# Joining Q and the selection in one DMA transpose, pairing the score rows of batch 0, and reordering the loads of a chunk-selecting attention kernel

## The chip, the cores and the metric

The kernel runs on one core of a Trainium2 chip. The metric is device time in microseconds (us) of one execution; each figure below is the median of several executions, with the range where it matters. Every execution has a state; nearly all of those here are fast, the few slow ones are left out of the ratios, and only fast runs are compared. Engine names: PE is TensorE's matmuls and PEld its weight loads, DVE is VectorE, ACT is ScalarE, POOL is GpSimd, SP is SyncE, which issues most of the transfers. The profile itself is one execution, so its span differs by a microsecond or two from the median.

## The reference

Four batches, eight heads, 768 positions, head size 64. K is cut into 24 chunks of 32 positions. For each query an upper bound of its score with each chunk is formed from the chunk's minimum and maximum, and only the best six chunks are attended to. The result goes through a gated feed-forward layer.

```python
k_min, k_max = k_chunks.min(axis=3), k_chunks.max(axis=3)
ub = sum(maximum(q * k_min, q * k_max), axis=-1)          # 24 bounds for each query
ub = where(causal, ub, -1e9)
top_chunks = argsort(ub)[..., -6:]
scores = where(chunk_of_key in top_chunks and key <= query, q @ k.T / 8, -1e9)
x = softmax(scores) @ v                                   # 3072 tokens x 512
out = (relu(x @ w_gate) * (x @ w_val)) @ w_out            # 512 -> 1536 -> 512
```

## The kernel before

The work is split into 16 attention jobs, one for each batch and pair of heads, and six feed-forward units of 512 tokens. The two are interleaved, so that TensorE does feed-forward matmuls while the other engines prepare the next job. The first 128 positions of each batch need no selection and form a "first block" of their own.

A planner written in Python orders every operation before the program is built. It simulates the engines with estimated costs and takes, whenever an engine comes free, the ready operation of best priority. The order that results is fixed: each engine then works through its queue in order. An operation that waits holds up everything behind it in that queue, so a wrong estimate in the planner becomes a real wait on the chip.

```python
op("SP", 1.25, prio, f, after=after, makes=makes, take=take, hold=hold, lag=2.6)  # a DMA transpose
...
if ok and (best is None or (ops[i][2], i) < (ops[best][2], best)):                # the choice: by priority
    best = i
```

In this form a DMA transpose is, for the planner, 1.25 us of SyncE and a result 2.6 us later; it does not take time on the DMA queue, although loads do (an operation on "DMA").

The mask of the selection is added by TensorE itself. A score matmul contracts 128 rows: 64 rows of K against Q, and in the other 64 rows a one-hot table of chunks, `ind`, with a large negative value, against the transposed "not selected" flags. Both operands of it, `kx[h]` and `qx[h]`, are therefore put together from halves:

```python
for h in range(2):                                  # K: two half copies for a job
    copy_half(eng[h], n, ..., kx[h][64*h:64*h+64], kT, h, ...)
for h in range(2):                                  # Q: two half copies
    copy_half(eng[h], n, ..., qx[h][64*h:64*h+64], qT, h, ...)
sT = turned(sn, ..., lambda: sel, nr, on_pe, ...)   # the selection, transposed
for h in range(2):                                  # and copied to the other halves
    copy_half(eng[h], nr*128, ..., qx[1-h][64*h:64*h+64], sT, h, ...)
...
nc.tensor.matmul(t[:, h, o:o+m*128], kx[h][:, c*128:(c+1)*128],
                 qx[h][:, (qb-1)*128:(qb-1+m)*128], ...)
```

K, Q and the attention output x are transposed on TensorE in batches 0 and 1 and by DMA in batches 2 and 3; the selection too. K and Q of batches 0 and 1 are loaded in long runs (eight positions of a head in one piece), those of batches 2 and 3 in short ones (one position). The feed-forward weights come in four equal groups, issued by GpSimd:

```python
WIDE = lambda b: b < 2            # long runs
PE_KQ = PE_SEL = PE_X = lambda b: b < 2
for i in range(4):
    weights(("w", i), [gate part i, value part i], (-28.0, -7.9, -7.8, -7.7)[i],
            after=[(("ld","v",-1),("ld","q",0),("ld","q",1),("ld","q",2))[i]])   # a landing
for i in range(4):
    weights(("wo", i), [output part i], (4.0, 5.0, 6.0, 7.0)[i], after=[("ld","v",3)])
```

The softmax here doesn't subtract the row's maximum and nothing guards it: scores larger than these inputs give would overflow.

## Time and profile before

| | before |
|---|---|
| median of 4 runs | 309.53 us (308.92 to 310.26) |
| profiled execution, span | 308.1 us |
| TensorE busy | 274.3 us |
| VectorE, ScalarE, GpSimd busy | 184.3, 178.1, 91.9 us |

The profile of before, first part: busy time of each engine, with its share of the span and its instructions.

```profile
PE 274.3 (89%) x2230; PEld 148.5 (48%) x2268; DVE 184.3 (60%) x524; ACT 178.1 (58%) x242; POOL 91.9 (30%) x164
```

Second part of the same page: the span in 40 slices of 7.7 us. The digits are tenths: busy share of TensorE, its granted clock, busy share of the DMA engines.

```profile
PE   2841998967998998999999899999999999999994
...
PEclk9995899995999999999999999999999999999999
DMA  9999999999899779986662264231100110020002
```

TensorE is full from the eleventh slice on. Ahead of that it has holes, the DMA engines are full, and the granted clock falls to half twice: 22.6 to 32.8 us and 70.4 to 77.2 us in the trace's clock records. The Trainium skill, "TensorE: Matmul & The Clock Gate", Part 1, says that the clock is halved after an idle window of about 3.4 us; here the clock did fall (0.50 granted), but without a single hole that long ahead of it. The stretches are 10.24 and 6.83 us long, multiples of 3.41 us. In the 3.41 us before the first, TensorE was busy 1.17 us, and its longest hole was 1.5 us; in the 3.41 us before the second it was busy 0.82 us, and the holes there are 2.6 and 2.2 us long. The 6.0 us wait shown below falls inside the first stretch. So shorter holes close together were enough. What they cost is their idle time and the work at half clock after them.

Stretches of before. Columns: the stretch and its length; busy time and instructions of PE, PEld, DVE, ACT, POOL; mean granted clock; DMA share (the time that packets took, over the time of 16 engines; packets overlap, so it can pass 1); GB/s.

```profile
0.00:80.00 80.00, 56.09 (x521) 32.29 (x530) 50.85 (x150) 39.69 (x53) 40.54 (x68) 0.89 1.20 210
80.00:120.00 40.00, 37.02 (x366) 21.45 (x371) 36.74 (x96) 33.56 (x47) 19.34 (x33) 1.00 0.92 180
120.00:180.00 60.00, 57.69 (x576) 33.89 (x585) 52.16 (x178) 47.97 (x61) 22.42 (x43) 1.00 0.69 129
180.00:220.00 40.00, 39.68 (x391) 23.02 (x396) 23.01 (x74) 31.18 (x40) 9.54 (x23) 1.00 0.33 70
220.00:320.00 100.00, 83.80 (x382) 37.83 (x387) 21.51 (x32) 25.67 (x43) 0.00 (x0) 1.00 0.09 34
```

TensorE idles 23.9 us of the first 80, 3.0 of the next 40 and 2.3 of the 60 after that. The last row runs past the end of the span (308.1), so its idle time is 88.1 - 83.8 = 4.3 us.

What TensorE waited for in before: total us, times, longest.

```profile
PE g L793 <- DMA wg_61<-in_moe_w_gate_dram: 6.0, 1, 6.0
...
PE yp L828 <- DMA wo_69<-in_moe_w_out_dram: 2.6, 1, 2.6
PE yp L828 <- DMA wo_70<-in_moe_w_out_dram: 2.2, 1, 2.2
```

The timeline of before, TensorE and then GpSimd: start, length, engine and line, instruction, and in brackets the wait ahead of it.

```profile
30.17 1.48 PE L793 MATMUL g<-xT,wg_61 128*128 128x512 bf16 x3 [5.96 <-DMA wg_61<-in_moe_w_gate_dram]
...
68.38 0.82 PE L828 MATMUL yp<-wo_69,hT 128*128 128x512 bf16 x3 [2.59 <-DMA wo_69<-in_moe_w_out_dram]
...
16.84 0.91 POOL L850 DMA_DIRECT2D wg_61<-in_moe_w_gate_dram  x1
...
57.58 0.76 POOL L850 DMA_DIRECT2D wo_69<-in_moe_w_out_dram  x1
```

The first gate weights are issued at 16.84 us and are awaited until 30.17; the first output weights are issued at 57.58 and awaited until 68.38. The Trainium skill, "DMA: Bandwidth & Descriptors", section "Issuing engines are not separate DMA queues", says that transfers run on the same 16 engines and interleave whichever engine issued them. That fits the trace: the weights, issued by GpSimd, took 12.9 us to land beside SyncE's loads, while the DMA share stood at 1.2.

### The profile page before, as it was taken

What the parts mean: (1) busy time and instruction counts of PE and PEld (TensorE: products, weight loads), DVE (VectorE), ACT (ScalarE), POOL (GpSimd) and SP (SyncE); (2) the same over time, 40 slices, a digit from 0 to 9 for tenths busy, and PEclk for the clock granted to TensorE, in tenths of its full rate; (3) what the DMA queues carried; (4) which work ended last, traced back from release to release, by engine and by line L of the source; (5) the groups of instructions that cost most, each with busy time, mean ns of one, the idle gap of its engine ahead of it and who ended that gap; (6) DMA issues with size and microseconds to landing.
All of it is one profiled execution on the core that took longest, in us unless ns stands there. A gap on an engine that the chain in (4) does not pass through costs nothing.

```text
span 308.1 us, 5930 instructions
## 1 busy us (share of the span) xinstructions
PE 274.3 (89%) x2230; PEld 148.5 (48%) x2268; DVE 184.3 (60%) x524; ACT 178.1 (58%) x242; POOL 91.9 (30%) x164
## 2 busy tenths in 40 slices
PE   2841998967998998999999899999999999999994
PEld 1431455643565554555655455555544444444441
DVE  7454789952879999978998798523434023204310
ACT  3421378860979794877898788988233223233321
POOL 5594146670555263243533332223000000000000
PEclk9995899995999999999999999999999999999999
DMA  9999999999899779986662264231100110020002
GB/s 168 218 229 222 212 214 227 209 187 231 158 235 242 90 172 186 187 145 137 168 139 49 56 89 80 92 80 54 24 0 0 69 70 0 34 104 1 0 34 102
DMA packets 95389, 37.88 MB, mean 123 GB/s; under 512 B 83840, under 2 KB 89472, under 8 KB 95360
## 3 DMA queue, kind: packets, MB, share of 16 engines
q1 hardware_dynamic: 89536, 32.78, 53.5%
q0 software_dynamic: 5824, 4.72, 9.6%
q8 instruction: 17, 0.28, 0.4%
q14 instruction: 12, 0.10, 0.1%
HBM read 30.41 MB, written 6.29 MB: 119 GB/s over the span
## 4 chain that ended last, share of the span: by engine, by line
PE 58%; DMA 19%; POOL 6%; DVE 5%; issue 5%; ACT 3%; SPq 2%; POOLq 0%; ACTq 0%; DVEq 0%
PE g L793 20%; PE yp L828 19%; DMA vraw<-in_v_dram 7%; PE sT L675 7%; PE vl L793 6%; PE o L726 5%; DMA kraw<-in_k_dram 5%; DMA wo_70<-in_moe_w_out_dram 3%; DMA qT<-qbf 2%; DMA kT<-kbf 2%; POOL aT L698 2%; DVE kmm L552 1%; SPq L380 1%; ACT aT L686 1%; POOL kbf L521 1%
## 5 line engine op out<-in xcount | busy, mean ns | idle before, releaser
L686 ACT ACTIVATE aT<-sT 128x1024 bf16<-128x1024 f32 x80 | 78.7, 1022 | 20.7 <-PE sT L675 16.7
L804 ACT ACTIVATE grl<-g 128x512 bf16<-128x512 f32 x72 | 42.9, 596 | 58.5 <-PE g L793 50.3
L698 POOL TENSOR_SCALAR_AFFINE_SELECT aT<-aT 128x256 bf16<-128x256 bf16 x80 | 32.2, 417 | 63.5 <-ACT aT L686 63.1
L812 DVE TENSOR_TENSOR hT<-vl,grl 128x512 bf16<-128x512 f32 x48 | 33.1, 689 | 21.3 <-PE vl L793 20.2
L828 PEld LDWEIGHTS <-hT 128*128 128x128 bf16 x288 | 27.7, 99 | 37.2 <-issue 3.8
L812 DVE TENSOR_TENSOR hT<-g,grl 128x512 bf16<-128x512 f32 x24 | 16.6, 692 | 45.3 <-ACT grl L804 31.6
L552 DVE TENSOR_REDUCE kmm<-kT 128x24 bf16<-128x768 bf16 x32 | 29.8, 948 | 7.4 <-PE kT L343 7.2
L838 ACT ACTIVATE y<-yp 128x512 f32<-128x512 f32 x24 | 14.4, 598 | 27.3 <-PE yp L828 23.3
L675 PEld LDWEIGHTS <-kx_all 128*128 128x128 bf16 x256 | 21.5, 98 | 14.3 <-issue 1.3
L726 PEld LDWEIGHTS <-aT 128*128 128x128 bf16 x640 | 23.2, 98 | 9.3 <-POOL aT L698 2.7
L793 PE MATMUL g<-xT,wg_61 128*128 128x512 bf16 x69 | 18.5, 390 | 6.1 <-DMA wg_61<-in_moe_w_gate_dram 6.0
L828 PE MATMUL yp<-wo_69,hT 128*128 128x512 bf16 x71 | 19.9, 386 | 3.0 <-DMA wo_69<-in_moe_w_out_dram 2.6
L828 PE MATMUL yp<-wo_70,hT 128*128 128x512 bf16 x70 | 20.3, 400 | 2.2 <-DMA wo_70<-in_moe_w_out_dram 2.2
L828 PE MATMUL yp<-wo_71,hT 128*128 128x512 bf16 x70 | 19.2, 379 | 0.2
L828 PE MATMUL yp<-wo_72,hT 128*128 128x512 bf16 x70 | 19.0, 379 | 0.1
L793 PE MATMUL g<-xT,wg_63 128*128 128x512 bf16 x70 | 18.2, 379 | 0.9 <-ACT grl L804 0.8
L521 POOL CAST kbf<-kraw 96x1024 bf16<-96x1024 f32 (+1 forms) x16 | 15.2, 952 | 11.6 <-DMA kT<-kbf 5.1
L363 DVE COPY kx_all<-kT 64x768 bf16<-64x768 bf16 x24 | 18.2, 759 | 0.4
L793 PE MATMUL g<-xT,wg_62 128*128 128x512 bf16 x70 | 18.2, 379 | 0.2
L793 PE MATMUL g<-xT,wg_64 128*128 128x512 bf16 x69 | 18.2, 379 | 0.1
L521 POOL CAST qbf<-qraw 80x1024 bf16<-80x1024 f32 (+1 forms) x16 | 14.1, 882 | 13.4 <-DMA qT<-qbf 11.5
L741 DVE TENSOR_TENSOR x<-o,zr 128x320 bf16<-128x320 f32 x32 | 15.7, 491 | 1.1
(187 smaller groups left out, 449.7 us busy)
## 6 DMA issues: line engine op xcount, KB each, us to landing
kraw<-in_k_dram SPq DMA_DIRECT2D x16, 384.0 KB, 7.6
vraw<-in_v_dram SPq DMA_DIRECT2D x16, 384.0 KB, 6.4
out_dram<-y SPq DMA_DIRECT2D x24, 256.0 KB, 2.0
qraw<-in_q_dram SPq DMA_DIRECT2D x8, 320.0 KB, 12.2
qraw<-in_q_dram SPq DMA_DIRECT2D x16, 160.0 KB, 3.7
kraw<-in_k_dram SPq DMA_DIRECT2D x4, 256.0 KB, 5.0
qraw<-in_q_dram SPq DMA_DIRECT2D x4, 256.0 KB, 5.0
vraw<-in_v_dram SPq DMA_DIRECT2D x4, 256.0 KB, 5.1
```

Of the source, the lines that this page charges most:

```text
L363: nc.vector.tensor_copy(out=out, in_=i)
L521: nc.gpsimd.tensor_copy(out=new(nm + "bf", bn)[0:np_, 0:ns * 2 * D].rearrange("p (r h d) -> p r h d", h=2, d=D), in_=TL[rn][0:np_, 0:ns * ...
L552: nc.vector.tensor_reduce(out=TL[mm][:, m], in_=i, axis=AX.XY if wide else AX.X, op=o)
L675: nc.tensor.matmul(t[:, h, o:o + m * 128], kx[h][:, c * 128:(c + 1) * 128], qx[h][:, (qb - 1) * 128:(qb - 1 + m) * 128], start=(si == 0), ...
L686: nc.scalar.activation(out=TL[an][:, :, a0:a0 + w], in_=TL[sn][:, :, 0:w], func=ACT.Exp, scale=scale)
L698: nc.gpsimd.affine_select(out=d, in_=d, compare_op=ALU.is_ge, fill=0.0, base=0, channel_multiplier=-1, pattern=[[0, 2], [1, 128]])
L726: nc.tensor.matmul(TL[on][:, r - 1, h - h0, :], TL[an][:, h, o:o + 128], vb[:, h, c, :], start=(i == 0), stop=(i == NP - 1))
L741: nc.vector.tensor_tensor(out=TL[xn][:, :, h0 * D:(h0 + hs) * D].rearrange("p r (h d) -> p r h d", d=D), in0=TL[on][:, :, :, 0:D], in1=TL[ ...
L793: nc.tensor.matmul(ps, w[:, kt, cs], TL[xn][:, kt, :], start=(kt == 0), stop=(kt == KT_ - 1))
L804: nc.scalar.activation(out=new("grl", rn), in_=g, func=ACT.Relu)
L812: nc.vector.tensor_tensor(out=TL[hn][:, nt, :], in0=vv, in1=TL[rn], op=ALU.mult)
L828: nc.tensor.matmul(TL[pn], TL[hn][:, nt, tl * 128:(tl + 1) * 128], wo_sb[nt // NPG][:, nt % NPG, :], start=(nt == 0), stop=(nt == NTI - 1))
```

## The change

The intent is to take copies from VectorE and ScalarE, to fill TensorE's holes at the start, and to make the planner's idea of the DMA queue true. The parts:

1. *Start.* Weight groups of 2, 3, 3 and 4 tiles instead of four of 3; each is released by the issue of a load plus a delay instead of a landing; V of the first blocks comes later; the output weights come in two transfers instead of four.
2. *Pair* (batch 0). K, Q and the selection are copied whole. The scores become two passes of matmuls on half the array's height: K against Q, then `ind` against the selection, one head on each half of the rows.
3. *Join* (batches 1 to 3). GpSimd casts Q into a tile `cb` beside the selection, and one DMA transpose of ten 128x128 blocks writes `qx` directly. No copy of Q or of the selection is left there. K, Q (for the clamps of the bound) and x of batch 1 are still transposed on TensorE.
4. *Loads.* K and Q of batch 1 in short runs like those of batches 2 and 3; Q loads all six blocks in one transfer. x goes into one circular tile.
5. *Planner.* A transpose now takes 0.144 us for each block on the planner's DMA queue; SyncE's operations cost 0.12 us more; transfers are taken in the order in which they become available. It also counts the loads in flight in finer units (six, of which a short-run load takes three; before three, of which it took two).

The core of the diff, with cuts:

```diff
+        if eng == "SP":
+            cost += 0.12
 ...
+                    rank = (at[i] if eng in flow else ops[i][2], i)
 ...
-    WIDE = lambda b: b < 2
+    WIDE = lambda b: b < 1
+    PAIR = lambda b: b < 1
-    PE_SEL = lambda b: b < 2
+    PE_SEL = lambda b: b < 1
 ...
+    WGS = [2, 3, 3, 4]
+    xT = const.tile([128, KT_, XC * 128], BF16)
+    cb_l = [const.tile([128, NQ, 2, 128], BF16, name=f"cb{i}") for i in range(NCB)]
 ...
-            op("SP", 1.25, prio, f, after=after, makes=makes, take=[(tag, name)], hold=hold,
-               lag=2.6)
+            dma_t(nr, prio, f, after, makes, take=[(tag, name)], hold=hold)
+    def dma_t(nr, prio, f, after, makes, take=(), hold=()):
+        made = makes[0]
+        op("SP", 1.25, prio, f, after=after, makes=[("ti", made)], take=take, hold=hold, lag=0.0)
+        op("DMA", 0.144 * nr, prio, None, after=[("ti", made)], makes=makes, ...)
 ...
+            if nm == "q" and not PAIR(b):
+                def f_cb(cb=cb, rn=rn):
+                    for h in range(2):
+                        nc.gpsimd.tensor_copy(out=cb[:, :, h, h * D:h * D + D], in_=src[:, h, 1:])
 ...
+        else:
+            dma_t(2 * NQ, p, lambda: nc.sync.dma_start_transpose(
+                out=qx.rearrange("f r h p -> f (r h) p"), in_=cb...), ...)
 ...
+                if PAIR(b):
+                    for k_, q_, first in ((kx[0], x[:, 0:SQ], True), (ind, x[:, SQ:], False)):
+                        for si, (c, qb, m) in enumerate(bank):
+                            for h in range(2):
+                                hs = slice(64 * h, 64 * h + 64)
+                                nc.tensor.matmul(t[:, h, o:o + m * 128],
+                                                 k_[hs, c * 128:(c + 1) * 128],
+                                                 q_[hs, (qb - 1) * 128:(qb - 1 + m) * 128], ...)
 ...
-                (-28.0, -7.9, -7.8, -7.7)[i], [(("ld","v",-1),("ld","q",0),("ld","q",1),("ld","q",2))[i]])
+                ..., [(("iss","v",-1),("iss","k",0),("iss","v",0),("iss","v",1))[i]], 1.5 if i == 0 else 3.5)
```

## The prediction

> **What bounds the kernel now.** The table of stretches shows two regimes. From 80 us on TensorE is busy 218.2 of 228 us: it is the bound. Before 80 us it is busy only 56.1 us, with a granted clock of 0.50 around 24-32 and 72-76 us, while the DMA share stays at its ceiling (1.18-1.22, about 210 GB/s). So about 24 us, and half-clock time, are lost to loads. The timeline and the waits name the holes: the first gate weights are issued at 16.8 us and land 12.9 us later, so TensorE waits 6.0 us until 30.2 and job 0's selection, behind it in order, runs only at 35.3; the first output weights are issued at 57.6 us, behind a V cast that waits 5.0 us for its load; TensorE idles around 65.7-71.4, then runs at half clock till about 78. From 80 to 120 us VectorE is busy 36.7 and ScalarE 33.6 of 40 us, and 3 us of TensorE idle come from their chain.
>
> **What changes.**
> - Load order and weights: a first weight group of 2 tiles (2/3 of the bytes), gated by the issue of loads instead of a landing; K and Q before V; output weights in two transfers, issued earlier. At the rate of before (about 1.5 MB in 19 us) the first group lands near 23 us instead of 30-32. I estimate 7 us earlier, and most of the 65.7-71.4 hole with its half-clock tail (4-8 us) gone. Against it, batch 1's K and Q are now loaded in short runs, and twelve Q loads bring 384 KB instead of 320.
> - VectorE: batch 0's half copies become whole copies (4 x 0.76 saved), selection copies fall from 10.6 to about 2 us, Q copies (3.2) and half the clamps (2.6) leave; memsets add 2. Net -16 us. ScalarE: Q and selection copies leave (about -20), clamps come (+5.6): about -14. GpSimd: 24 casts into the joined tile, about 0.4 each from the 0.72 us of a 128x640 cast: about +10 on 92.
> - TensorE: 20 selection transposes leave (55 ns apart, -1.1 us). Batch 0's scores become two passes of half-height matmuls. The trace has such pairs: at full clock eight started 30 ns apart, so two run together. But entering costs: the first half-height matmul started 0.45 us after the previous 512-column one, where 0.216 is usual. The Trainium skill, "TensorEngine Tiling (Array Packing)", Key Properties, says a change of tiling mode drains the array; the trace agrees. About 16 entries at 0.2-0.3: +3 to 5 us (estimate).
> - DMA: joined transposes move 10 blocks instead of 5; a 5-block one took 2.7 us to land. I expect 4-6 us, mostly planned for.
>
> **On the critical path.** Start: -8 to -13 us. Middle, through VectorE and ScalarE: -2 to -3. TensorE's own work: +2 to +4. Sum about -9.5.
>
> **Prediction:** 300.5 us, 80% range 293 to 307. Faster by over 2%: 0.70; within 2%: 0.26; slower: 0.04.
>
> **What would show it.** Right: the first gate matmul starts near 23-25 us; the first output matmul waits for weights under 1 us; TensorE's busy time before 80 us rises from 56 to about 66; VectorE total near 168, ScalarE near 164, GpSimd near 102; TensorE's busy time about 275-279; idle after 120 us no larger. Wrong: batch 0's scores taking over 5 us more; TensorE waiting on the joined transpose between 70 and 120 us; GpSimd casts on the chain.
>
> **What would make it wrong.** If the load ceiling only moves the hole later (short-run K and Q crowding out weights), the start gains 3-4 us and the result is about 306. If drains cost little and the start fills fully, 293.

## The result, and the profile after

| | before | after |
|---|---|---|
| median of 4 runs each | 309.53 us | 301.85 us (301.73 to 302.26) |
| ratio, with 95% interval | | 0.9753 (0.9727 to 0.9779) |
| profiled execution, span | 308.1 us | 300.6 us |
| TensorE busy | 274.3 us | 273.4 us |
| VectorE, ScalarE, GpSimd busy | 184.3, 178.1, 91.9 us | 168.3, 162.5, 98.0 us |

A ratio here and below is the mean time of one kernel's fast runs over the mean of the other's fast runs of the same rounds on the same chip, so it is not quite the ratio of the medians. The change makes the kernel 2.5% faster, 1.35 us above the predicted median.

The profile after, first part, and the slices (now 7.5 us each):

```profile
PE 273.4 (91%) x2258; PEld 145.6 (48%) x2292; DVE 168.3 (56%) x482; ACT 162.5 (54%) x222; POOL 98.0 (33%) x186
...
PE   2975796998999999989979899999999999999995
...
PEclk9999998999999999999999999999999999999999
DMA  9999999999799999999999622322000020020002
```

While TensorE works, the half clock is down to one stretch, 50.5 to 53.9 us. The DMA engines, however, now stay full until slice 22 (165 us), where before they had eased from slice 19 on (139 us).

Stretches of after, same columns:

```profile
0.00:80.00 80.00, 62.74 (x663) 34.77 (x671) 55.53 (x165) 44.62 (x59) 44.88 (x81) 0.98 1.15 207
80.00:120.00 40.00, 39.39 (x395) 23.28 (x400) 34.48 (x104) 28.39 (x40) 20.43 (x39) 1.00 1.26 217
120.00:180.00 60.00, 55.11 (x589) 32.78 (x596) 47.40 (x165) 47.39 (x60) 28.68 (x58) 1.00 1.09 180
180.00:220.00 40.00, 39.74 (x269) 20.19 (x273) 12.25 (x23) 18.82 (x26) 3.97 (x10) 1.00 0.20 52
220.00:320.00 100.00, 76.44 (x349) 34.61 (x354) 18.68 (x27) 23.28 (x39) 0.00 (x0) 0.99 0.08 32
```

Read the two tables row by row. TensorE's idle time in the first 80 us falls by 6.65 us. From 80 to 120 us it falls from 3.0 to 0.6; of the waits named there in before, 1.7 us were for copies by VectorE and ScalarE into `kx` and `qx`, and they are gone. From 120 to 180 us it rises from 2.3 to 4.9, and the DMA share rises in the same row from 0.69 to 1.09.

What TensorE waited for in after:

```profile
PE sT L741 <- DMA qx_93<-cb_97: 1.8, 1, 1.8
...
PE sT L741 <- DMA qx_91<-cb_95: 1.5, 2, 1.4
...
PE sT L741 <- DMA qx_92<-cb_96: 1.3, 2, 1.1
```

`sT` are the scores and `qx<-cb` are the joined transposes. Asked of 120 to 180 us alone, the same view lists nothing else: 1.8, 1.5 and 1.1 us, together 4.4 of the 4.9 us that TensorE idles there. These waits did not exist before.

The timeline after, TensorE and GpSimd:

```profile
21.54 1.02 PE L866 MATMUL g<-xT,wg_61 128*128 128x512 bf16 x3
...
36.15 0.39 PE L731 MATMUL sT<-qx_91,kx_all 64*128 64x512 bf16 x2
36.38 0.38 PE L731 MATMUL sT<-qx_91,ind 64*128 64x512 bf16 x2
...
76.48 1.46 PE L901 MATMUL yp<-wo_69,hT 128*128 128x512 bf16 x5
...
13.03 0.89 POOL L923 DMA_DIRECT2D wg_61<-in_moe_w_gate_dram  x1
...
50.94 0.84 POOL L923 DMA_DIRECT2D wo_69<-in_moe_w_out_dram  x1
```

The first gate matmul starts 8.6 us earlier; its weights, a smaller group, land 5.2 us after their issue instead of 12.9. The first output matmul does not wait for weights any more. The half-height matmuls come in pairs: two of 512 columns, one for each head, every 0.22 us.

The transfers without a size in the page's list of issues are the transposes; the last number is the median time from issue to landing. In before:

```profile
kT<-kbf SPq DMA_TRANSPOSE x8, 3.4
qT<-qbf SPq DMA_TRANSPOSE x8, 2.6
...
selT<-sel_78 SPq DMA_TRANSPOSE x3, 2.7
```

In after:

```profile
kT<-kbf SPq DMA_TRANSPOSE x8, 4.3
qT<-qbf SPq DMA_TRANSPOSE x8, 4.2
...
qx_93<-cb_97 SPq DMA_TRANSPOSE x4, 4.2
qx_91<-cb_95 SPq DMA_TRANSPOSE x4, 4.1
```

The joined ones land in 4.1 to 4.2 us (a third group of four, left out here, also in 4.2), and the transposes of K and Q, whose size is the same in the two kernels, have also become slower.

The chain that ended last, from 110 to 172 us of after: start, length, what. Only its transfers are copied.

```profile
110.56 6.06 DMA qx_92<-cb_96
...
129.17 5.63 DMA qx_91<-cb_95
...
146.57 5.40 DMA qx_93<-cb_97
...
156.72 3.62 DMA qx_91<-cb_95
...
166.13 3.48 DMA qx_92<-cb_96
```

These five pieces are 24.2 us of the chain. That is not idle time of TensorE, which does feed-forward work meanwhile; it shows through what the next job's scores come: VectorE's comparison, the joined transpose, the scores, and no copy in between.

Where the 7.5 us between the two profiled spans came from:

| term | measured | how |
|---|---|---|
| idle time before 80 us | -6.65 us | first rows |
| work done at half clock | -2.7 us | busy time at clock 0.50 was 8.9 us, is 3.4; half of the difference (estimate) |
| TensorE's own work, at full clock | +1.9 us | busy time less half of what ran at half clock: 269.8, then 271.7 |
| idle time, 80 to 220 us | +0.15 us | three rows: -2.4, +2.6, -0.1 |
| after 220 us, idle | -0.15 us | last rows, less what lies past the span |

The split is coarse. The ends of matmuls are modelled in the trace, and some records are missing: before's trace has 2230 matmuls, e1's 2268, for the same TensorE work. By the working of the third row, e1 (below) comes to 273.1 us, 3.2 us more than before without any new work on TensorE. A difference of 2 us in that row is therefore no evidence of a cause, and the idle rows share the doubt.

### The profile page after: what moved, and what is told of

Read it like the earlier page. It is cut to its first block, busy times and chain, and to the rows that moved or that the text cites. A ratio compares the mean times of both kernels' runs of the same rounds, so it can differ in the third digit from the quotient of the medians.

```text
span 300.6 us, 5925 instructions
## 1 busy us (share of the span) xinstructions
PE 273.4 (91%) x2258; PEld 145.6 (48%) x2292; DVE 168.3 (56%) x482; ACT 162.5 (54%) x222; POOL 98.0 (33%) x186
## 4 chain that ended last, share of the span: by engine, by line
PE 70%; DMA 18%; DVE 5%; issue 2%; POOL 2%; ACT 1%; SPq 0%; POOLq 0%; ACTq 0%; DVEq 0%
PE g L866 23%; PE yp L901 19%; PE vl L866 9%; PE sT L741 7%; PE o L793 6%; DMA qraw<-in_q_dram 5%; DMA kraw<-in_k_dram 5%; DMA qx_92<-cb_96 3%; DMA qx_91<-cb_95 3%; DMA qx_93<-cb_97 2%; PE sT L731 2%; DVE hT L885 1%; PE kT L367 1%; PE xt L367 1%; PE ub L651 1%
## 5 line engine op out<-in xcount | busy, mean ns | idle before, releaser
L753 ACT ACTIVATE aT<-sT 128x1024 bf16<-128x1024 f32 x80 | 79.6, 1026 | 23.4 <-PE sT L741 15.7
L901 PE MATMUL yp<-wo_70,hT 128*128 128x512 bf16 x141 | 34.8, 379 | 0.2
L901 PE MATMUL yp<-wo_69,hT 128*128 128x512 bf16 x137 | 34.3, 379 | 0.4
L741 PEld LDWEIGHTS <-kx_all 128*128 128x128 bf16 x192 | 16.0, 98 | 17.8 <-DMA qx_91<-cb_95 2.5
L866 PE MATMUL g<-xT,wg_64 128*128 128x512 bf16 x91 | 24.1, 379 | 0.2
L550 POOL CAST kbf<-kraw 128x768 bf16<-128x768 f32 (+1 forms) x16 | 14.4, 898 | 14.1 <-DMA kraw<-in_k_dram 11.5
L866 PE MATMUL g<-xT,wg_63 128*128 128x512 bf16 x71 | 18.3, 379 | 0.2 <-issue 0.2
L866 PE MATMUL g<-xT,wg_62 128*128 128x512 bf16 x70 | 18.2, 379 | 0.1
L801 DVE RECIPROCAL zr<-o 128x5 f32<-128x5 f32 x32 | 6.1, 190 | 20.5 <-PE o L793 20.5
L866 PE MATMUL vl<-xT,wv_68 128*128 128x512 bf16 x61 | 16.1, 379 | 0.2
L550 POOL CAST qbf<-qraw 128x640 bf16<-128x640 f32 (+1 forms) x16 | 13.0, 810 | 9.2 <-DMA qraw<-in_q_dram 9.2
L625 ACT ACTIVATE qmn<-qT 128x640 bf16<-128x640 bf16 x16 | 11.5, 722 | 7.2 <-PE qT L367 6.2
L866 PEld LDWEIGHTS <-wg_64 128*128 128x128 bf16 x96 | 8.9, 98 | 10.7 <-issue 1.3
```

The source lines that it names most:

```text
L550: nc.gpsimd.tensor_copy(out=new(nm + "bf", bn)[0:np_, 0:(ns - r0) * 2 * D].rearrange("p (r h d) -> p r h d", h=2, d=D), in_=TL[rn][0:np_, ...
L741: nc.tensor.matmul(t[:, h, o:o + m * 128].rearrange("k (r p) -> k r p", p=128), kx[h][:, c * 128:(c + 1) * 128], qx[:, qb - 1:qb - 1 + m, ...
L753: nc.scalar.activation(out=TL[an][:, :, a0:a0 + w], in_=TL[sn][:, :, 0:w], func=ACT.Exp, scale=scale)
L866: nc.tensor.matmul(ps, w[:, kt, cs], xT[:, kt, xc:xc + 512], start=(kt == 0), stop=(kt == KT_ - 1))
L901: nc.tensor.matmul(TL[pn], TL[hn][:, nt, tl * 128:(tl + 1) * 128], wo_sb[nt // NPG][:, nt % NPG, :], start=(nt == 0), stop=(nt == NTI - 1))
```

## The experiments

The first question was what made the gain. Theory A: the new start, because TensorE's idle time fell there. Rival B: the copies taken from VectorE and ScalarE. Rival C: the planner's new accounting, which changes no work at all. The second question came up with the rows of 120 to 180 us: does the join pay for itself, or do its transposes return what it saves? All twelve kernels gave correct results, and all edits are to after unless said otherwise. The runs were made on four chips in four groups (e1 to e4, e5 to e8, e9 to e11, e12); before was run in every group, with medians of 309.26, 309.17, 310.23 and 309.76 us, and kernels of different groups are compared by their ratios to it.

| kernel | median, us | ratio to before (95%) |
|---|---|---|
| after | 301.85 | 0.9753 (0.9727 to 0.9779) |
| e1: before, new start only | 312.95 | 1.0104 (1.0031 to 1.0176) |
| e2: after, old start | 304.40 | 0.9841 (0.9788 to 0.9894) |
| e3: no join; long-run loads in batch 1 | 307.04 | 0.9917 (0.9860 to 0.9974) |
| e4: no pair | 302.43 | 0.9751 (0.9696 to 0.9807) |
| e5: pair in batches 0 and 1, no join | 306.24 | 0.9906 (0.9868 to 0.9943) |
| e6: pair in batches 0 and 1, join from 2 | 309.47 | 0.9999 (0.9963 to 1.0036) |
| e7: old accounting in the planner | 318.83 | 1.0314 (1.0274 to 1.0354) |
| e8: e6, batch 2's K and Q turned on TensorE | 310.92 | 1.0051 (1.0018 to 1.0084) |
| e9: no join; loads as in after | 298.49 | 0.9629 (0.9594 to 0.9664) |
| e10: e6, loads in order | 310.46 | 1.0008 (0.9958 to 1.0059) |
| e11: only the transposes' queue time undone | 313.78 | 1.0115 (1.0069 to 1.0160) |
| e12: no pair, no join | 303.79 | 0.9816 (0.9763 to 0.9870) |

The expectations below use letters of their own: S is theory A, R is rival B, and their C, in e5 and e6, is not rival C. Many missed. S failed in e1 and e3; e2 came out just above R's range, e4 between its two ranges, e5 where J put it, and e6 and e9 outside both of theirs, e9 on the fast side. In e7, e8, e10, e11 and e12 the second of the two ranges, or the larger effect, came true.

### e1: the new start alone

```diff
 (to the kernel before)
-    WG = 4
+    WGS = [2, 3, 3, 4]
-            op("SP", 0.6, -40.0 + b, f_ld, ...)                         # loads of the first blocks
+            op("SP", 0.6, -40.0 + b + (1.5 if nm == "v" else 0.0), f_ld, ...)
-    weights(...), [(("ld","v",-1),("ld","q",0),("ld","q",1),("ld","q",2))[i]])
+    weights(...), [(("iss","v",-1),("iss","k",0),("iss","v",0),("iss","v",1))[i]], 1.5 if i == 0 else 3.5)
+    (output weights in two transfers)
```

> The kernel before with only the new start: weight groups of 2, 3, 3 and 4 tiles, weights gated by issues, V of the first blocks after K and Q, two transfers of output weights. Theory S (the gain is the earlier weights): ratio to before 0.975 to 0.985, first gate matmul near 22 us, no hole of TensorE before the first output matmul. Rival R (the gain is the relief of VectorE and ScalarE; new loading only moves the hole): ratio above 0.99.

It came out 1.0% slower than before. Its stretches:

```profile
0.00:80.00 80.00, 64.56 (x618) 36.93 (x619) 56.78 (x158) 45.91 (x62) 42.14 (x70) 0.98 1.20 215
80.00:120.00 40.00, 30.87 (x322) 19.04 (x321) 34.07 (x90) 26.91 (x37) 16.23 (x28) 0.91 0.90 183
```

And TensorE's waits from 78 to 92 us:

```profile
PE selT L345 <- ACT qx L363: 3.1, 1, 3.1
PE o L728 <- DVE kx_all L365: 1.5, 1, 1.5
```

The start is filled even better than in after (64.6 us busy before 80 us), and nothing is gained: the hole comes back after 80 us, where TensorE waits for ScalarE's and VectorE's half copies, and the half clock with it. From 80 to 88 us VectorE is busy 7.86 of 8 us and TensorE 3.19. So theory A in its simple form is wrong: here an earlier start brought jobs sooner to engines that could not take them sooner.

### e2: after with the start of before

```diff
-    WGS = [2, 3, 3, 4]
+    WGS = [3, 3, 3, 3]
     (first blocks' V at its old place, weights released by landings, four output transfers)
```

> The kernel after with the start of before put back (four equal weight groups, gated by landings, V in turn with K and Q, four output-weight transfers); the planner's queue accounting stays. Theory S: about 306 to 309 us, most of the gain lost. Rival R: 301 to 304 us.

The ratio is 0.9841 against 0.9753, so inside after the new start is worth 0.9%, about 2.7 us. Together with e1, the same edit loses 1.0% in one kernel and gains 0.9% in the other. The first row of its stretches says where:

```profile
0.00:80.00 80.00, 63.75 (x683) 36.22 (x684) 58.25 (x170) 43.48 (x57) 44.74 (x79) 0.91 1.13 201
```

With the old start, and the first gate matmul at 28.5 us, TensorE is as busy before 80 us as in after (62.74); only its clock is lower, 0.91 against 0.98. So the fall of the idle time there does not need the new start: in e1 the new start brings it about alone, here the rest of the change does.

### e3: the join undone, first try

```diff
-    WIDE = lambda b: b < 1
+    MODE = ['pair', 'old', 'old', 'old']
+    WIDE = lambda b: b < 2
-    PE_SEL = lambda b: b < 1
+    PE_SEL = lambda b: b < 2
     (batches 1 to 3: half copies of Q and of the selection, two clamps as before)
```

> The kernel after with batches 1 to 3 in the form of before: Q and selection apart, each half copied by ScalarE or VectorE, batch 1 loaded in long runs and its selection turned on TensorE. Theory S, with the reading that the joined transposes give back between 120 and 180 us what they save between 80 and 120: 300 to 303 us, equal to after within 0.7%, no wait of scores on a joined transpose, VectorE total up by about 12 us. Rival R: 305 to 309 us.

The ratio of 0.9917 looked as if the join were worth 1.6%. That reading was wrong. The edit also brought back the long-run loads of batch 1. In the planner those count little or nothing against the number of transfers in flight (one credit for K, none for Q, three for the short ones), so they went out ahead of the V loads of batch 0: between 28 and 49 us SyncE issues one V load in e3 and three in e9. The run changed two things and settles nothing about the join; e9 repeats it with the loads held fixed.

### e4: the pair undone

```diff
+    MODE = ['old', 'join', 'join', 'join']
     (batch 0: half copies, full-height scores; all else as in after)
```

> The kernel after with batch 0 in the old form (half copies of K, Q and selection, full-height score matmuls, no change of tiling mode), all else as after. If the pairs' entries and exits (about 0.1 us each by the trace, 16 of each) outweigh 5 us less on VectorE: 299 to 301 us. If the relief outweighs them: 303 to 305 us. TensorE's busy time should fall by 2 to 3 us against after, VectorE's rise by about 5.

The ratio, 0.9751, is after's. Beside the join, the pair is worth nothing that these runs can tell. TensorE's busy time was to fall by 2 to 3 us against after and did not (274.1 us; 270.7 at full clock, worked out as above, 1.0 less than after); VectorE's rose by 3.6.

### e5 and e6: the pair in batch 1 too, without and with the join

```diff
 e5
+    MODE = ['pair', 'pair', 'old', 'old']
+    WIDE = PE_SEL = lambda b: b < 2
 e6
+    WIDE = PAIR = PE_SEL = lambda b: b < 2          # join from batch 2
```

> The kernel after, with batches 0 and 1 both in the paired form (whole copies, half-height score matmuls, long-run loads, selection turned on TensorE) and batches 2 and 3 in the form of before: no joined transpose anywhere, but VectorE and ScalarE relieved where the early start puts the load. Theory C (the start fills holes only if VectorE and ScalarE are relieved between 60 and 120 us; the start alone moves the hole there): TensorE busy between 80 and 120 us 38.5 or more of 40, about 301 to 303 us, 4 to 6 us less than the run with batches 1 to 3 in the old form (307.0). Rival J (the joining itself, with its fewer steps between selection and scores, is what gains): 306 to 308 us.

> The kernel after with batch 1 paired as batch 0 is, and joined only from batch 2 on. Theory C with the contention reading (batch 1's joined transposes and short-run loads are what fills the DMA queues from 80 to 160 us and makes scores wait 4.6 us there): 298 to 300.5 us, waits of scores on joined transposes under 2 us, DMA share between 80 and 120 us about 1.0 instead of 1.26. If the drains of paired scores (about 0.2 us a bank, 20 banks more, up to 4 us) eat it: 301.5 to 304 us.

Both are slower than after: e5 is 0.9% faster than before, e6 equal to it. One wait stands out in e6:

```profile
PE o L793 <- POOL vb L537: 5.9, 1, 5.9
```

`vb` is V cast to bf16, and GpSimd in turn waits 6.6 us for the load of V. In e6's timeline of SyncE's queue, one V load is issued at 32.13 us and four more only from 50.17 us on:

```profile
50.17 21.61 SPq L524 DMA_DIRECT2D vraw<-in_v_dram  x4
```

In after's, three V loads are issued from 29.04 us on, and another at 50.76. It is the flaw of e3: with long-run loads in batch 1, that batch's K and Q pass the V loads of batch 0. In e5 the same wait is 4.5 us. A version that pairs more batches cannot be judged by these two runs.

### e7: the planner's accounting undone

```diff
-            cost += 0.12
+            cost += 0.0
-                    rank = (at[i] if eng in flow else ops[i][2], i)
+                    rank = (ops[i][2], i)
-        op("SP", 1.25, prio, f, ..., lag=0.0)
-        op("DMA", 0.144 * nr, prio, None, after=[("ti", made)], makes=makes, ...)
+        op("SP", 1.25, prio, f, after=after, makes=makes, take=take, hold=hold, lag=2.6)
```

> The kernel after with the planner's accounting of before for DMA transposes (fixed 2.6 us after issue, no share of the queue), no added issue cost, and loads taken by priority. If the accounting only tidies the order: 301.5 to 303.5 us. If it is what makes the joined transposes bearable: above 305 us, with waits of scores on them over 8 us.

Not one instruction's work differs from after; only the order does. The time rises to 1.0314 of before, 5.6% of it above after, some 17 us, the largest effect of any edit here. TensorE waits 6.3 us for joined transposes (over 8 were expected) and 7.3 us for `aT`, the exponentials that GpSimd masks. This is rival C, given the join and the pair, and it is far larger than I had allowed for: the prediction only said that the transposes were "mostly planned for".

### e8: more transposes on TensorE

```diff
 (to e6)
-    PE_KQ = lambda b: b < 2
+    PE_KQ = lambda b: b < 3
```

> Batch 1 paired, and K and Q of batch 2 also turned on TensorE instead of by DMA (44 DMA blocks less, 44 matmuls of 55 ns more, 2.4 us). If DMA transposes of batch 2 are what scores wait for between 120 and 180 us: 1 to 2 us less than the same kernel with K and Q of batch 2 turned by DMA. If TensorE is the bound there: 1 to 2 us more.

It is 0.5% slower than e6 in the same rounds, which the intervals barely tell apart. Taking transposes from the DMA queue and giving them to TensorE does not help this version.

### e9: the join undone, with the loads as in after

```diff
+    MODE = ['pair', 'old', 'old', 'old']
     WIDE = lambda b: b < 1                          # as in after: batch 1 in short runs
-    PE_SEL = lambda b: b < 1
+    PE_SEL = lambda b: b < 2
-            if nm == "q" and not PAIR(b):
+            if nm == "q" and JOIN(b):               # never: no cast into cb
+        elif OLD(b):
+            sT = turned(sn, "T" if on_pe else "tT", lambda: sel_l[j % NSEL], nr, on_pe, p, ...)
+            (two half copies of the selection, two of Q)
```

> The unjoined run again without its flaw: there batch 1's long-run loads, which the planner lets go out uncounted, stood in the queue ahead of three V loads of batch 0. Here batch 1 is loaded in short runs as in after, so the first 40 loads stand in after's order; batches 1 to 3 keep the separate, half-copied form of before. Theory O (the order of the one load queue with the honest accounting is the gain; joining is worth little): 301 to 303.5 us. Theory J (joining is worth about 5 us): 305.5 to 308 us.

This is the fastest kernel: 298.49 us, 3.7% faster than before; its interval lies wholly below after's. Its stretch from 120 to 180 us, to be held against the third rows above:

```profile
120.00:180.00 60.00, 59.19 (x568) 34.06 (x576) 54.06 (x171) 50.64 (x66) 20.50 (x41) 1.00 0.69 129
```

And what TensorE waited for in that stretch, the whole answer:

```profile
PE vl L898 <- DVE hT L917: 0.3, 1, 0.3
```

Its transposes:

```profile
kT<-kbf SPq DMA_TRANSPOSE x8, 2.8
qT<-qbf SPq DMA_TRANSPOSE x8, 2.7
```

VectorE (54.1 of 60 us) and ScalarE (50.6) are busier here than in after (47.4 each), and TensorE does not wait for them. With the join they have time to spare and TensorE waits 4.4 us for the DMA queue. The profiled spans differ by 3.6 us (300.6 and 297.0), the busy times of TensorE by 0.1 us. So in this kernel the join costs about 3.5 to 4 us. That is the join as a whole: twelve transposes of ten blocks in place of eight of five, the extra casts on GpSimd, and batch 1's selection by DMA instead of on TensorE.

K's and Q's transposes, of the same size and number in both, land in 2.8 and 2.7 us here and in 4.3 and 4.2 us in after. It is tempting to say that the joined transposes slow every other one in the queue. The record does not show that. e12, which has no joined transpose either, has these:

```profile
kT<-kbf SPq DMA_TRANSPOSE x8, 3.5
qT<-qbf SPq DMA_TRANSPOSE x8, 4.2
```

And in e9 itself the three transposes of K between 80 and 120 us, beside many loads, took 4.8 us. What else the queue holds at the time matters, and the runs do not separate it from the joined transposes.

### e10: e6 with the loads in order

```diff
 (to e6)
-            dq = [... for i in range({"k": 1, "q": 0}[nm] if big else 3)]
+            dq = [... for i in range({"k": 1, "q": 0}[nm] if big and b < 1 else 3)]
```

> Batch 1 paired as before in the 309.5 us run, but its K and Q loads counted against the queue like all others, so that they stand behind batch 0's V loads. Theory O: the hole at 64.5 to 71.4 us (5.9 us, scores times V waiting for a V cast) goes, 299 to 302.5 us. If pairing batch 1 is itself the loss (drains): 305 us or more.

The wait for `vb` is gone, and TensorE is busy 13.83 us of the 14 from 66 to 80 us, yet the time stays at that of before. The loss has moved: TensorE is busy only 34.5 us of 40 from 80 to 120 and 56.0 of 60 from 120 to 180, with 5.5 us of waits for `aT` in the whole run. So the order of the loads explains e6's hole but not e6's time. Why pairing batch 1 does not pay stays open.

### e11: only the queue time of the transposes undone

```diff
-        op("SP", 1.25, prio, f, after=after, makes=[("ti", made)], take=take, hold=hold, lag=0.0)
-        op("DMA", 0.144 * nr, prio, None, after=[("ti", made)], makes=makes, ...)
+        op("SP", 1.25, prio, f, after=after, makes=makes, take=take, hold=hold, lag=2.6)
```

> Of the three parts of the planner's accounting, only the transposes are put back to 2.6 us after issue outside the queue; the added issue cost and first-come order of transfers stay, and the first 28 loads stand as in after. If the transposes' queue time is what the accounting is worth: 308 us or more, with scores waiting over 6 us on joined transposes. If first-come order of loads is: under 304 us.

The ratio rises to 1.0115, about 11 us above after, so the queue time of transposes is most of what e7 showed. TensorE's first wait now is:

```profile
PE sT L739 <- DMA qx<-cb: 9.6, 4, 4.2
```

With the old assumption, 2.6 us after issue however many blocks and whatever else is in the queue, the planner places the scores too early, and TensorE, which works in order, stands still at them four times. With the rest of the change as it is, the join without this accounting makes the kernel slower than before.

### e12: neither pair nor join

```diff
+    MODE = ['old', 'old', 'old', 'old']
     WIDE = lambda b: b < 1
+    PE_SEL = lambda b: b < 2
```

> All four batches in the separate, half-copied form of before: no pair, no join. What is left of the change is the start (weight groups and gates, V after K and Q), batch 1's loads in short runs, the circular tile and the planner's accounting. Theory O (order and accounting are the whole gain; pairing gives nothing that is not in the idle of VectorE and ScalarE): 298 to 300.5 us, 0.96 to 0.97 of before. Rival (the pair of batch 0 is needed to let the start fill): 303 us or more, with TensorE waiting on copies between 40 and 100 us. The same start on the kernel before without the accounting gave 1.0104.

The ratio is 0.9816; one of its six runs was slow and is left out. It completes a square, with the new start, the accounting and the loads of after in all four:

| | no join | join (batches 1 to 3) |
|---|---|---|
| batch 0 not paired | 0.9816 (e12) | 0.9751 (e4) |
| batch 0 paired | 0.9629 (e9) | 0.9753 (after) |

Without the join, the pair gains 1.9%, some 6 us; with it, nothing. With the pair, the join loses 1.2%; without it, the intervals of e12 and e4 overlap, so whether it gains is not shown. What can be said from the rows of the profiles: in e12 TensorE still waits for VectorE's half copies of the early jobs (2.8 us ahead of the bounds, 1.6 ahead of a transpose of the selection), and the pair copies K and the selection whole; in e9 1.5 us of the first wait are left and the second is gone. Both the pair and the join relieve the same two engines. Once the pair has done so where it mattered, the join's relief has nothing left to shorten, and its transposes remain as cost. The relief as the reason for this interplay fits the waits but is an argument; no run isolates it.

The square also answers the first question in part. e12 has the copies of before (VectorE 182.7 and ScalarE 177.2 us busy, before 184.3 and 178.1), and it is still 1.8% faster than before. So the start, batch 1's loads, the circular tile and the planner's accounting give most of the 2.5% of the whole change. The start alone lost 1.0% (e1), so the others together are worth 2.9% in a kernel without pair or join. Which of them does it was not separated: no run puts the accounting alone into before.

## Why the prediction was right, and where a term was off

The prediction said 300.5 us (293 to 307) and the result is 301.85. Point by point:

| step | predicted | measured |
|---|---|---|
| start, idle and half clock | -8 to -13 us | -9.4 us (-6.65 and -2.7) |
| middle, through VectorE and ScalarE | -2 to -3 us | +0.15 us |
| TensorE's own work | +2 to +4 us | +1.9 us |
| sum | about -9.5 us | -7.5 us between profiles |

**The start: right in size, wrong in the cause that it names.** The first gate matmul starts at 21.5 us (predicted 23 to 25), the first output matmul no longer waits for weights, and TensorE's busy time before 80 us rises to 62.7 (predicted 66). But the prediction gave the whole term to "load order and weights". e1 and e2 show that the weights' part by itself gains nothing in before and about 2.7 us in after, and that e2, with the old start, has lost none of the gain in idle time before 80 us (16.25 us idle, after 17.26, before 23.91). What of the rest is due to batch 1's loads, to the pair and to the planner was not separated term by term; e7 shows that, given the join, the planner's order alone carries more than the whole gain.

**The middle: the mis-sized term.** "Middle, through VectorE and ScalarE: -2 to -3" holds for 80 to 120 us alone, where idle time fell by 2.4 us. The prediction also said "idle after 120 us no larger", and that failed: it grew by 2.6 us from 120 to 180 us, to 4.9 us, and the joined transposes are the named wait for 4.4 of these. I had looked for that wait between 70 and 120 us, where it is 0.2 us, and had taken the copies as the only thing that changes on the way to the scores. In fact a short queue for copies was exchanged for a longer one for the DMA. The engine totals were right (VectorE 168.3 for 168, ScalarE 162.5 for 164, GpSimd 98.0 for 102), as was the landing time (4.1 to 4.2 us for 4 to 6); here right totals went with a wrong term, because a total does not say which engine a stage waits for. e9 puts the price of the join at 3.5 to 4 us.

**TensorE's own work: the number agrees, the reason is not shown.** The row gives +1.9 us, just under the range; the busy time itself, 273.4 us, lies below the 275 to 279 of the prediction. I had allowed 0.2 to 0.3 us for each entry into the half-height mode. The Trainium skill, "TensorEngine Tiling (Array Packing)", Key Properties, says that a change of mode drains the array. The starts of the matmuls in after's trace agree: going in costs 95 ns above the usual spacing (15 cases, 92 to 98) and coming out 92 ns (12 cases without another gap), together 0.19 us; with 16 such stretches that is about 3 us (estimate), less the 1.1 us predicted for the twenty transposes of the selection that left TensorE. That this makes the +1.9 us is not shown: by the same working the pair costs 1.0 us between e4 and after and nothing between e12 (271.9) and e9 (271.6), and e1, without it, already stands at 273.1. The same section says that different tiles work in parallel; the pairs of half-height matmuls, two of 512 columns every 0.22 us, show it.

**What the prediction did not see.** It treated the planner's edits as bookkeeping. The accounting of the transposes is worth about 11 us, given the join, and all of it about 17 us. The prediction was right because the change carries its own accounting along, not because that was costed; and its start term named the weights for a gain that e2 shows mostly without them. To that extent the close number is luck.

## What to carry to other kernels

In a kernel whose order is fixed ahead, an edit is worth what it does together with the order that is made for it: the same new start lost 1% in one kernel and gained 0.9% in the other, and a planner that did not know of the shared queue cost about 11 us given the join (e11), more than the 7.7 us that the whole change gained. Before moving copies from compute engines to a DMA transpose, ask which of the two queues the next stage waits for in that stretch; here VectorE could be busy 54 of 60 us without being waited for, while at a DMA share of 1.09 TensorE waited 4.4 us. The share alone does not tell: from 80 to 120 us it stood at 1.26, and TensorE waited 0.2 us for the joined transposes. And when a part is undone to measure it, keep the order of the loads the same: the first try at undoing the join (e3) gave the opposite sign of the careful one (e9).

## What the Trainium skill lacked or had wrong

- "TensorEngine Tiling (Array Packing)", Key Properties, says that a change of mode drains the array but gives no size. Here 95 ns to go in and 92 ns to come out, beside 512-column matmuls of 216 ns each.
- "Advanced Engine Details and Errata", section X-Bar Transpose (TRN2), says that transposing transfers are as fast as regular ones, and expects 350 to 400 GB/s. Here a joined transpose of ten blocks (0.33 MB) landed 4.1 to 4.2 us after its issue, about 80 GB/s counted so, and one of five blocks (0.16 MB) in 2.6 us, about 63. These times hold all latency and the queueing beside loads, so they do not refute the rate, but a planner needs the landing time, and no page gives one for several blocks in a shared queue.
- No page says how long a transpose takes to land beside others and beside loads. Here the medians for K and Q, eight transposes each of one size, were 3.4 and 2.6 us in before, 4.3 and 4.2 in after, 2.8 and 2.7 in e9, 3.5 and 4.2 in e12. Whether bytes, packets or the order of issue do it was not tested.
- "TensorE: Matmul & The Clock Gate", Part 1, ties the half clock to an idle window of about 3.4 us, and gives no busy share below which a window counts as idle. Here the half clock (0.50) came after 3.41 us in which TensorE was busy 1.17 and 0.82 us (before) and 1.23 us (after, up to 50.5 us, where its longest idle piece was 1.8 us).
